# RWKV-6 attention with a hard-swish feed-forward on one core: the u sums of two chunks made wide, weights stored by partition, and a new instruction order

## The chip, the cores and the metric

One core of one Trainium2 chip runs the program. The metric is device time in microseconds; the runs of the kernel before are 543.66, 543.9 and 544.48 us, median 543.9 us.

## What is computed

The reference is a recurrence per batch entry and head, followed by a two-layer feed-forward over 3072 tokens:

```
batch, n_heads, seq, head_dim = (4, 8, 768, 48)
...
    for t in range(S):
        cur = np.einsum('bhd,bhe->bhde', u[None] * kt, vt)
        y[:, :, t] = np.einsum('bhd,bhde->bhe', rt, state + cur)
        state = wt[:, :, :, None] * state + np.einsum('bhd,bhe->bhde', kt, vt)
...
    h = x @ w_in
    g = h * np.clip(h + 3.0, 0.0, 6.0) / 6.0
    return (g @ w_out).astype(np.float32)
```

r, k, v, w and u are float32; w_in and w_out come as float64 and are sent to the core as 64-bit words.

## The kernel before

The sequence is cut into 24 chunks of 128 tokens (`L`), each of two halves of 64 (`HL`). Four chunks make a block of 512 tokens, so there are six blocks. Within a chunk the recurrence becomes matrix products:

- VectorE makes two running products of the decays (`back_scan`, L429, and `fore_scan`, L438) and with them scaled keys K (`make_k`, L449) and scaled reads R (`make_r`, L453).
- TensorE multiplies K by R for each half and head (`score`, L499). The part above the diagonal goes into the matrix A by a masked copy on VectorE (`above`, L506).
- The diagonal of A is the sum over d of r*k*u, which is what the reference's u term needs. For chunks 0 to 8, VectorE multiplies r by k (`own`, L462), TensorE multiplies by u (`own_dot`, L474: eight matmuls of 2 columns into a 128x8 tile), ScalarE copies the eight sums (`own_sum`, L480), and ScalarE scales the identity `eyes` by each of them (`diagonal`, L490, eight instructions of 128x64, in two steps of four).
- TensorE turns K (`turn_k`, L515; copied by `turned_k`, L520), adds keys times values to the state (`write`, L599; copied by `written`, L610, or L608 for chunk 1), and reads the old state (`read_state`, L577) and the values (`read_values`, L586) into y.
- For chunks 0 and 1 the last 16 rows of each head pair go round through x: `clear_y` (L650), `read_both` (the step "first"), `leave_last` on ScalarE (the step "third", L644 and L642), and `place_last` (L658, the step "read"). `leave_rest` copies y to x. For later chunks `leave` (L682) does it.

The feed-forward of block 0 is made directly (`up` L715, `ramp` L705, `gate` L726, `down` L734). For blocks 1 to 5 it goes by sums of parts and fewer products: sums of weights (`sum_w` and `sum_out`, L777 to L806) and of x (`sum_x`, the steps tx), products (L830), their reads on VectorE (L847) or ScalarE, `clip` (L851), a gate (L855), and the second layer (L885).

Weights arrive as 64-bit words in tiles `bits`, 768 KB at a time (`fetch`, L392, sixteen of them; w_in in three pieces of 2 KB for each partition, w_out in two of 3 KB). ScalarE makes two steps of each (`low_whole` L401, `high_sign` L406), VectorE two (`high_shift` L412, `high_low` L416, the step "full"). All loads of features, tokens and weights are issued by SyncE in one queue.

All of this is one order, written down as a table. `plan.add` names every step with its engine, a cost, what it must follow and which buffers it holds; `Plan.order` (L183) sorts the steps by the table `ORDER`, two characters for each step. Costs don't choose the order any more: they only give planned starts, and those decide how many filler matmuls `Plan.emit` (L231) puts before a TensorE step of the first 60 us (`spin`, L1257, 128 columns of the identity into a bank that nobody reads; four more stand ahead of everything). An engine runs its steps strictly in this order.

Of the kernel before, what the change touches and what calls it, by code (L numbers as in the profile page):

```python
# [31 lines left out]
ALONE = 4  # L32
LEAD = 5.403
# [49 lines left out]
    "AAADAIAQAKAOALANAPARASAYAVAjATAXAZAdAmAqAfAoAzA3A/ACAFAWAiAcAnAbAaAeAgAhAlAtAyAkApAxA1A5A9A8A+BNBUBcAJAMBIBfBSBaBRBF"  # L83
    "BJBTBVBXCGCLBpBvCBCRBdCYCdCnCyC7AUAvBjB4BuCABzBeBgBlBmBqCSCaCJCOCWCrCNCuC1E0DCDMDVDgBOBQCpC2DcDkCvCUCbCiDDDXDuDyC+DH"
    "DjFFDKFMFQFUFfFnFwCXDLC9DGEOEZDBDADRDWDsEKFzDZDqFPFWE5FZFeFkF3GVGXGlGfCcC4D9EJFmFpEEDYDwD+F2F5GYFlFvFoGNGPGSGiG0G5Do"
    "FxETFyF+GDEXEDFXFcGhGjG6F7GdF8GrGzG2HPHYHkH0HsEdGaF4GZGxG1F9FdGWGgHAHCHcGnHHGoHMHOHRH/IEIIFrG8FuGkG7HXHhGqGcGpHbHeIJ"
    "HVHiHWHyH2H9IrJWJlJtJ0GHHdGIG/HmItIyHGGtHNIPIVJcIDINIHIYIcKMLfLkG3IKG9HzILI/JCH3HZHjJeJjLnIvJbIwJgJiLxMAMLMWMQHnJdHo"
    "JvJ4K/LDJ1IBIdLqLuMIKTLtLwL1MRMfMmI4LlI6KHLmL6MBKOJUJnMFMPMpL4MJMbMiMwOvO9PEPLLHMGLKLrMHMZMeLyLZL0MtMxO5MYMrL9MvMzM6"
    "PJP+QKLSMnLVMNMoNANHMUL2MTO2PIQCM4O8M3PoPpPsQWQdQiQyQqNYO4NaOSO3PXPbOYN5OFQBQGQjPPQJPQQNQQQXQ5RIRQOCQEOEPhQDQcQgPlOg"
    "PRQrQwRUQbQvQeQxQ0Q1R3SoS1S6TCOHQkOKQIQlRERLQSPUQMRZRcSwQ+RWRARgRjRnTlUdUlRNRRRVRqRwSISNRvR/SOSuS9UiR7SzR8ULUNUPUvU9"  # L90
    "VOVUVYSCSvSETATWT+UCTISeSpUqUtVDTsUhTqUnUpUuVWVhVqSUUkSXTgUjU8VATkSyTGVCVKVsU1VHU6VLVPVVWAYTYVYjYZShVESnUrVFVbVfUxTL"
# [1510 lines left out]
```

## Time and profile before

| | |
|---|---|
| runs, us | 543.66, 543.9, 544.48 (median 543.9) |
| profiled execution, us | 544.22 |
| its span, first to last instruction | 542.5 us |
| TensorE busy | 533.3 us (98%) |
| VectorE, ScalarE, GpSimd busy | 425.6, 267.6, 113.1 us |
| granted TensorE clock | 0.999 of full |

The span is what the trace covers; the execution's own time is 1.7 us longer. Busy time of TensorE counts fillers, and the ends of its matmuls are modelled, so a wait that is shorter than the pipeline does not show as idle. Where a row reads "idle before, releaser", the engine had nothing until the named instruction ended.

### The profile page before, as it was taken

Reading aid. Unit: us, or ns where it says so; the run is one execution under the profiler, and the core shown is the slowest. Engines: PE = TensorE matmul, PEld = TensorE weight load, DVE = VectorE, ACT = ScalarE, POOL = GpSimd, SP = SyncE. Lnnn points to the kernel's source line nnn. Section 1 sums busy time; section 2 is a strip of 40 time slices with the busy share of each in tenths; the row PEclk is TensorE's granted clock in tenths of the full one; section 3 lists DMA queues with packets and bytes.
Section 4 is the critical chain, followed back from the end, with each engine's and each line's share of the span. In section 5 each row is a group of like instructions: output and inputs, shape, how many; then the busy total and the mean of one; then the engine's idle time right before and its main releaser. Section 6 shows DMA issues by size and latency. Waiting matters only on the chain.

```text
span 542.5 us, 13407 instructions
## 1 busy us (share of the span) xinstructions
PE 533.3 (98%) x5558; PEld 467.9 (86%) x5558; DVE 425.6 (78%) x726; ACT 267.6 (49%) x657; POOL 113.1 (21%) x111
## 2 busy tenths in 40 slices
PE   8999999999999999999999999999999999999995
PEld 8888876666878999888999888999888999888995
DVE  7889999768999977999977999968889624478531
ACT  4999894333664333556424657425454324264200
POOL 2000002456230135212513154115310000000000
PEclk9999999999999999999999999999999999999999
DMA  8959753333342343745145853032510001000001
GB/s 297 359 165 346 245 176 105 125 119 125 99 151 68 105 159 110 232 177 184 26 137 160 302 217 127 0 118 87 171 59 1 2 16 31 30 0 2 1 29 36
DMA packets 23670, 66.45 MB, mean 122 GB/s; under 512 B 3216, under 2 KB 10544, under 8 KB 23600
## 3 DMA queue, kind: packets, MB, share of 16 engines
q1 hardware_dynamic: 23472, 65.50, 35.4%
q8 instruction: 46, 0.75, 0.6%
q14 instruction: 24, 0.20, 0.1%
q10 hardware_dynamic: 128, 0.00, 0.0%
HBM read 59.69 MB, written 4.72 MB: 119 GB/s over the span
## 4 chain that ended last, share of the span: by engine, by line
PE 92%; DVE 6%; issue 1%; POOL 0%; ACT 0%; DVEq 0%; POOLq 0%
PE bank L885 29%; PE bank L830 24%; PE bank L715 8%; PE bank L734 8%; PE bankS L885 5%; PE bankS L830 4%; PE y_ps L577 2%; PE bankS L1261 2%; PE ps L515 2%; PE y_ps L599 2%; PE bank L499 2%; PE y_ps L586 2%; DVE g L847 2%; DVE g L855 1%; PE ps L474 1%
## 5 line engine op out<-in xcount | busy, mean ns | idle before, releaser
L851 ACT ACTIVATE clip<-g,three 128x512 f32<-128x512 f32 x80 | 57.1, 722 | 55.0 <-DVE g L847 45.3
L847 DVE TENSOR_TENSOR g<-bank,g 128x512 f32<-128x512 f32 x80 | 53.6, 684 | 10.0 <-PE bank L830 8.5
L855 DVE SCALAR_TENSOR_TENSOR g<-clip,g 128x512 f32<-128x512 f32 x80 | 56.5, 720 | 5.8 <-ACT clip L851 5.8
L885 PE MATMUL bank<-w_out,g 128*128 128x192 f32 x320 | 57.4, 328 | 0.0
L490 ACT ACTIVATE A<-eyes,dg 128x64 f32<-128x64 f32 x192 | 49.5, 338 | 10.9 <-PE y_ps L586 10.6
L885 PEld LDWEIGHTS bank<-w_out,g 128*128 128x128 f32 x320 | 52.8, 190 | 1.2 <-DVE g L855 0.3
L449 POOL TENSOR_TENSOR K<-feat_in,E 112x512 f32<-112x512 f32 x17 | 22.6, 1329 | 134.2 <-PE bank L499 128.4
L682 ACT COPY xT<-y_ps 48x256 f32<-48x256 f32 x88 | 32.1, 365 | 27.7 <-PE y_ps L586 26.9
L715 PE MATMUL bank<-xT,w_in 128*128 128x256 f32 (+1 forms) x216 | 45.5, 362 | 0.0
L734 PE MATMUL bank<-w_out,g 128*128 128x384 f32 x128 | 43.8, 491 | 0.0
L830 PE MATMUL bank<-xT,w_in 128*128 128x256 f32 x160 | 40.4, 381 | 0.1
L715 PEld LDWEIGHTS bank<-xT,w_in 128*128 128x128 f32 x216 | 36.6, 191 | 4.4
L845 ACT COPY g<-bank 128x512 f32<-128x512 f32 x50 | 28.8, 581 | 20.7 <-PE bank L830 17.2
L734 PEld LDWEIGHTS bank<-w_out,g 128*128 128x128 f32 x128 | 23.6, 190 | 14.1
L901 ACT ACTIVATE o<-bank 128x192 f32<-128x192 f32 x30 | 9.9, 329 | 49.8 <-PE bank L885 49.6
L830 PEld LDWEIGHTS bank<-xT,w_in 128*128 128x128 f32 x160 | 30.1, 190 | 4.4 <-ACT g L845 0.7
L429 DVE TENSOR_TENSOR_SCAN E<-feat_in,back 112x520 f32<-112x520 f32 x24 | 31.4, 1309 | 2.7 <-DMA feat_in<-in_feat_dram 1.7
L506 DVE COPY_PREDICATED A<-mask,bank 128x256 f32<-128x256 uint8 x48 | 18.6, 440 | 17.4 <-PE bank L499 17.3
L453 POOL TENSOR_TENSOR W<-feat_in,W 112x512 f32<-112x512 f32 x17 | 22.8, 1343 | 44.3 <-DVE W L438 44.3
L438 DVE TENSOR_TENSOR_SCAN W<-feat_in,start 112x520 f32<-112x520 f32 x24 | 31.4, 1309 | 0.6 <-PE y_ps L577 0.4
L830 PE MATMUL bank<-xT,bits 128*128 128x256 f32 x120 | 30.9, 382 | 0.2 <-DVE A L506 0.2
L885 PE MATMUL bank<-more,g 128*128 128x192 f32 x160 | 28.7, 329 | 0.0
(290 smaller groups left out, 1137.1 us busy)
## 6 DMA issues: line engine op xcount, KB each, us to landing
feat_in<-in_feat_dram SPq DMA_DIRECT2D x23, 772.5 KB, 4.4
bits<-in_moe_w_in_dram SPq DMA_DIRECT2D x8, 768.0 KB, 6.2
bits<-in_moe_w_out_dram SPq DMA_DIRECT2D x8, 768.0 KB, 4.9
feat_in<-in_moe_w_in_dram SPq DMA_DIRECT2D x8, 768.0 KB, 4.8
feat_in<-in_moe_w_out_dram SPq DMA_DIRECT2D x8, 768.0 KB, 4.7
rk_in<-in_tok_dram SPq DMA_DIRECT2D x15, 384.0 KB, 5.2
v_in<-in_tok_dram SPq DMA_DIRECT2D x24, 192.0 KB, 4.6
out_dram<-o SPq DMA_DIRECT2D x24, 192.0 KB, 2.1
```

The lines of the kernel that those rows point to most:

```text
L429: nc.vector.tensor_tensor_scan(out=E_[:, ::-1], data0=d["w"][:, :0:-1], data1=back.rearrange("q p t -> q (p t)")[:, ::-1], initial=0.0, op ...
L438: nc.vector.tensor_tensor_scan(out=W_, data0=d["w"][:, :-1], data1=starts[i % 2].rearrange("q p t -> q (p t)"), initial=0.0, op0=ALU.mult, ...
L490: nc.scalar.activation(out=d["A"][:, h, :], in_=eyes, func=ACT.Copy, scale=d["dg"][:, h])
L682: nc.scalar.copy(out=blocks[bk]["xT"][g * GP:g * GP + D, :, at:at + HL], in_=st[i]["y_ps"][a][(g ^ a) * GP:(g ^ a) * GP + D, :, :])
L715: nc.tensor.matmul(h_ps[:, :(c1 - c0) * L], lhsT=w_in[:, f // 2, j, f % 2, :], rhs=b["xT"][:, j, c0 * L:c1 * L], start=(j == 0), stop=(j = ...
L734: nc.tensor.matmul(b["o", c][:, :DM], lhsT=g_of(0, f, c), rhs=w_out[:, f, :], start=(f == 0), stop=(f == NFC - 1))
L830: nc.tensor.matmul(b["p", d, c][:, z * HB:(z + 1) * HB], lhsT=weight(W_PLACE[r], d)[:, z, :], rhs=x_at(bk, X_PLACE[r]), start=fresh and z ...
L845: nc.scalar.copy(out=out_, in_=src)
L847: nc.vector.tensor_tensor(out=out_, in0=src, in1=out_of(bk, d, other), op=ALU.add if sign > 0 else ALU.subtract)
L851: nc.scalar.activation(out=c, in_=out_of(bk, d, u), func=ACT.Relu, bias=three, scale=twice)
L855: nc.vector.scalar_tensor_tensor(out=g, in0=blocks[bk]["r", d, u], scalar=6.0, in1=g, op0=ALU.min, op1=ALU.mult)
L885: nc.tensor.matmul(b["d", p, to][:, :h], lhsT=a, rhs=w(), start=(f == 0 and k in (1, 5)), stop=(f == HF - 1 and k in (2, 3, 4)), skip_grou ...
```

## The change

Three things change in the program, and one in the order.

1. For chunks 0 and 1 (`BROAD`) the multiplication by u is made 128 columns wide: u is repeated 64 times, so that each sum stands in all 64 columns of its head. One VectorE multiplication by `eyes`, read out of PSUM, then makes the whole diagonal. ScalarE's copy and its eight scalings of these two chunks are gone.
2. The host stores w_in and w_out so that the 6 KB of a partition of one `fetch` lie together. Sizes are the same.
3. The rule for fillers: before a wait that is planned to be 1 us or more, fillers reach 0.3 us past the planned start, where they ended 0.12 us ahead of it before. The planner's costs are set to other numbers, and its transfer rate to 400 from 270.
4. `ORDER` is another table. `clear1` no longer waits for `kvs1`.

```
+BROAD = (0, 1)
 ORDER = (
-    "AAADAIAQAKAOALANAPARASAYAVAjATAXAZAdAmAqAfAoAzA3A/...
+    "AAACAHANAPARAMALAOAQAUAbASAWAYAaAjAqAdAoAvAzA+ADAE...
...
-    RATE = 270.0
+    RATE = 400.0
-    SPIN = ((6.3, 0.43), (1e9, 0.224))
-    FROM, UPTO = 3.0, 60.0
+    SPIN = ((7.2, 0.43), (1e9, 0.224))
+    FROM, UPTO, LONG = 3.0, 60.0, 1.0
...
-                while now < self.start[n] - 0.12:
+                room = -0.12 if self.start[n] < now + self.LONG else 0.3
+                while now < self.start[n] + room:
                     self.spin()
...
-                src = moe_w_in[:, f * 128:(f + 2) * 128].rearrange("(c p) (x j) -> p c x j", p=128, x=2)
+                src = moe_w_in[f // 2]
...
-                src = moe_w_out[f * 128:(f + 2) * 128, :].rearrange("(x p) (c j) -> p x c j", p=128, j=128)
+                src = moe_w_out[f // 2].rearrange("p x (c j) -> p x c j", j=128)
...
+        def broad_dot(i):
+            d = st[i]
+            d["dg_ps"] = pp.tile([L, P, 2, HL], F32, name="ps")
+            for p in range(P):
+                for a in range(2):
+                    half = slice(a * HL, (a + 1) * HL)
+                    nc.tensor.matmul(d["dg_ps"][half, p], lhsT=d["rk"][:, p, half],
+                                     rhs=u_col[:, p, :].rearrange("q (g o) -> q g o", o=1).to_broadcast([PR, 2, HL]),
+                                     start=True, stop=True)
+
+        def broad_diagonal(i):
+            d = st[i]
+            d["A"] = wk.tile([L, H, HL], F32, name="A")
+            nc.vector.tensor_mul(d["A"], d["dg_ps"].rearrange("s p g t -> s (p g) t"),
+                                 eyes.rearrange("s (o t) -> s o t", o=1).to_broadcast([L, H, HL]))
...
+            if i in BROAD:
+                plan.add(f"dot{i}", "PE", 0.95, do(broad_dot, i), [f"own{i}"], k + OWN, [("ps", [f"diag1{i}"])])
+            elif i < BY_PE:
...
+            if i in BROAD:
+                plan.add(f"diag1{i}", "DVE", 0.68, do(broad_diagonal, i), [f"dot{i}"] + [f"diag1{i - 1}"] * (i > 0), k + 0.6, [("A", [read_by(i)])])
...
-                plan.add(f"clear{i}", "PE", 0.5, do(clear_y, i), [f"kvs{i}", f"score{i}"], t, y)
+                plan.add(f"clear{i}", "PE", 0.95, do(clear_y, i), [f"kvs{i}"] * (i != APART) + [f"score{i}"], t, y)
...
-                plan.add(f"low{j}", "ACT", 0.83, do(low_whole, j), [f"fetch{j}"], t, [("more", [f"full{j}"])])
+                plan.add(f"low{j}", "ACT", 0.93, do(low_whole, j), [f"fetch{j}"], t, [("more", [f"full{j}"])])
...
-                plan.add(f"own{i}", "POOL", 2.2, do(own, i), [f"rkt{i}", "u"] + [f"own{i - 1}"] * (i > 0), k + 0.4,
+                plan.add(f"own{i}", "POOL", 2.4, do(own, i), [f"rkt{i}", "u"] + [f"own{i - 1}"] * (i > 0), k + 0.4,
...
-                plan.add(f"tx{bk}.{x}", "DVE", 0.335 * (X_PARTS[x + 1] - X_PARTS[x]), do(sum_x, bk, x),
+                plan.add(f"tx{bk}.{x}", "DVE", 0.44 * (X_PARTS[x + 1] - X_PARTS[x]), do(sum_x, bk, x),
...
-    laid["moe_w_in"] = _np.asarray(inputs["moe_w_in"])[rows]
+    w_in = _np.asarray(inputs["moe_w_in"])[rows]
+    laid["moe_w_in"] = w_in.reshape(nj, 128, -1, 2, 128).transpose(2, 1, 0, 3, 4)
+    laid["moe_w_out"] = _np.asarray(inputs["moe_w_out"]).reshape(-1, 2, 128, H * D).transpose(0, 2, 1, 3)
```

Line numbers of the changed kernel are some 2 to 24 higher: its narrow sums are L475, its wide sums L484, its VectorE diagonal L491, its fillers L1285.

SyncE's queue began with feat0 (the decays, then the rest), feat1, tok0, fetch0, tok1, fetch1, fetch2, feat2, and begins now with feat0, tok0, feat1, tok1, fetch2, fetch1, fetch0, feat2.

The first place is TensorE from the program's start. `ident` fillers are L1261 and L1285; `ps<-u_col,rk` is the u sum, `ps<-ident,K` the turning of K, `bank<-W,K` the scores. Before:

```order
L1261 MATMUL bankS<-ident 128x128 x17
L474 MATMUL ps<-u_col,rk 64x2 x8
L1261 MATMUL bankS<-ident 128x128 x3
L515 MATMUL ps<-ident,K 128x112 x4
L499 MATMUL bank<-W,K 64x64 x16
```

and now:

```order
L1285 MATMUL bankS<-ident 128x128 x12
L484 MATMUL ps<-u_col,rk 64x128 x8
L1285 MATMUL bankS<-ident 128x128 x4
L533 MATMUL ps<-ident,K 128x112 x4
L1285 MATMUL bankS<-ident 128x128
L517 MATMUL bank<-W,K 64x64 x16
```

Five fillers fewer stand before the first u sum, which is 128 columns wide instead of 2, and two more stand behind it. Over the whole program there were 17, 3, 2, 1, 3, 2, 3, 6 and 1 fillers in groups, 38 in all; there are now 12, 4, 1, 8, 2, 3, 1, 1 and 2, 34 in all. Up to the step read1 that is 37 before and 27 now.

The second place is VectorE after its constants, from the first scan on (`E<-feat_in,back` is the backward scan, `W<-feat_in,start` the forward scan, `rk` the product r*k, `top` and `w_in<-top,more` the steps shift and full). Before:

```order
L429 SCALAR_TENSOR_TENSOR E<-feat_in,back 112x520
L433 RECIPROCAL start_80<-E 112x8
L462 TENSOR_TENSOR rk<-feat_in 112x512
L438 SCALAR_TENSOR_TENSOR W<-feat_in,start_80 112x520
L449 TENSOR_TENSOR K<-feat_in,E 112x512
L506 COPY_PREDICATED A<-mask,bank 128x4x64 x2
L528 TENSOR_TENSOR S<-kvs,w_min 112x192
L453 TENSOR_TENSOR W<-feat_in,W 112x8x64
L544 TENSOR_TENSOR state_81<-S,kvs 112x192
L412 TENSOR_SCALAR top<-bits 128x768 x2
```

and now, from the product r*k of chunk 1 on:

```order
L463 TENSOR_TENSOR rk<-feat_in 112x512
L430 SCALAR_TENSOR_TENSOR E<-feat_in,back 112x520
L434 RECIPROCAL start_80<-E 112x8
L524 COPY_PREDICATED A<-mask,bank 128x4x64 x2
L413 TENSOR_SCALAR top<-bits 128x768
L450 TENSOR_TENSOR K<-feat_in,E 112x512
L491 TENSOR_TENSOR A<-ps,eyes 128x512
L546 TENSOR_TENSOR S<-kvs,w_min 112x192
L417 ISA w_in<-top,more 128x1536
L562 TENSOR_TENSOR state_81<-S,kvs 112x192
L439 SCALAR_TENSOR_TENSOR W<-feat_in,start_80 112x520
L413 TENSOR_SCALAR top<-bits 128x768
```

Both pieces are chunk 1. Its forward scan, and with it its R, stood right behind its backward scan and stand now behind the first finished piece of weights.

The third place is ScalarE from the copy of chunk 0's state part on (`more<-bits` are the steps low and sign, `kn<-ps` is turned, `xT<-y_ps` is third0). Before:

```order
L610 COPY kvs<-y_ps 112x384
L480 COPY dg<-ps 128x8
L490 ACTIVATE A<-eyes,dg 128x64 x8
L520 COPY kn<-ps 128x448
L401 ACTIVATE more<-bits 128x768
L406 ACTIVATE more<-bits 128x768
L644 COPY xT<-y_ps 48x128 x2
```

and now:

```order
L628 COPY kvs<-y_ps 112x384
L457 COPY w_min<-E 112x8
L402 ACTIVATE more<-bits 128x768
L407 ACTIVATE more<-bits 128x768
L402 ACTIVATE more<-bits 128x768
L538 COPY kn<-ps 128x448
L407 ACTIVATE more<-bits 128x768
L662 COPY xT<-y_ps 48x128 x2
```

Two pieces of weights, not one, now stand ahead of third0, and the scalings of the identity are gone.

## Rows read from the trace of the kernel before

**Rows 1.** The page's part 1: each engine's busy us, share of the span, instructions

```profile
PE 533.3 (98%) x5558; PEld 467.9 (86%) x5558; DVE 425.6 (78%) x726; ACT 267.6 (49%) x657; POOL 113.1 (21%) x111
```

**Rows 2.** Busy time by stretch: length, then each engine's busy us; clock, DMA share, GB/s

```profile
25.24:150.00 124.76, 124.52 (x1549) 94.28 (x1548) 109.08 (x212) 81.64 (x209) 30.39 (x27) 1.00 0.50 171
150.00:250.00 100.00, 99.25 (x939) 88.73 (x938) 90.35 (x136) 49.84 (x119) 26.61 (x24) 1.00 0.44 152
250.00:400.00 150.00, 149.37 (x1733) 136.31 (x1732) 128.65 (x204) 71.52 (x189) 51.67 (x46) 1.00 0.40 131
```

**Rows 3.** TensorE in order of time: start, length, line, tiles, records merged

```profile
7.49 0.63 PE L474 MATMUL ps<-u_col,rk 112*64 112x2 f32 x16
8.05 0.94 PE L1261 MATMUL bankS<-ident 128*128 128x128 f32 x6
8.82 0.55 PE L515 MATMUL ps<-ident,K 112*128 112x112 f32 x4
9.30 0.69 PE L499 MATMUL bank<-W,K 48*64 48x64 f32 x32
...
18.06 1.45 PE L658 MATMUL y_ps<-xT,S__115 112*128 112x64 f32 x12
...
23.80 1.60 PE L1261 MATMUL bankS<-ident 128*128 128x128 f32 x12
25.24 1.45 PE L658 MATMUL bank<-xT,S__115 112*128 112x64 f32 x12
```

**Rows 4.** The first fillers in two windows, 1.4 to 5.6 and 5.9 to 7.4

```profile
1.43 4.42 PE L1261 MATMUL bankS<-ident 128*128 128x128 f32 x19 [1.43 <-POOL ident masks.py:199]
...
5.65 1.91 PE L1261 MATMUL bankS<-ident 128*128 128x128 f32 x15
```

**Rows 5.** VectorE in order of time: chunk 0's product r*k, chunk 1's backward scan

```profile
6.38 0.67 DVE L462 TENSOR_TENSOR rk<-feat_in 112x512 f32<-112x512 f32 x1
...
8.99 1.24 DVE L429 TENSOR_TENSOR_SCAN E<-feat_in,back 112x520 f32<-112x520 f32 x1 [0.74 <-DMA feat_in<-in_feat_dram]
```

**Rows 6.** ScalarE in order of time, from chunk 1's scalings to third0

```profile
12.47 2.02 ACT L490 ACTIVATE A<-eyes,dg 128x64 f32<-128x64 f32 x8
14.39 0.52 ACT L520 COPY kn<-ps 128x448 f32<-128x448 f32 x1
14.80 1.09 ACT L401 ACTIVATE more<-bits 128x768 uint16<-128x768 uint32 x1
15.76 1.05 ACT L406 ACTIVATE more<-bits 128x768 bf16<-128x768 int32 x1
16.67 0.52 ACT L644 COPY xT<-y_ps 48x128 f32<-48x128 f32 x2
```

**Rows 7.** DMA issues at 2.2 us (tok0) and 3.2 us (tok1); last, us to landing

```profile
v_in<-in_tok_dram SPq DMA_DIRECT2D x1, 192.0 KB, 7.2
...
v_in<-in_tok_dram SPq DMA_DIRECT2D x1, 192.0 KB, 8.7
```

**Rows 8.** TensorE in order of time around 155 us, a wait and what follows

```profile
155.46 1.13 PE L830 MATMUL bank<-xT,apart 128*128 128x256 f32 x4 [0.46 <-DVE g L847]
156.42 1.03 PE L830 MATMUL bank<-xT,bits 128*128 128x256 f32 x4
```

**Rows 9.** Groups of VectorE, costliest first: busy us, mean ns, idle before

```profile
L847 DVE TENSOR_TENSOR g<-bank,g 128x512 f32<-128x512 f32 x80 | 53.6, 684 | 10.0 <-PE bank L830 8.5 <-ACT g L845 0.9
...
L429 DVE TENSOR_TENSOR_SCAN E<-feat_in,back 112x520 f32<-112x520 f32 x24 | 31.4, 1309 | 2.7 <-DMA feat_in<-in_feat_dram 1.7 <-POOL K L449 1.0
...
L726 DVE SCALAR_TENSOR_TENSOR g<-clip,bank 128x256 f32<-128x256 f32 (+1 forms) x36 | 13.4, 384 | 1.2 <-ACT clip L705 1.0
...
L482 DVE TENSOR_REDUCE dg<-rk 128x8 f32<-128x384 f32 x15 | 8.1, 542 | 1.3 <-ACT A L490 0.7 <-POOL rk L466 0.6
```

**Rows 10.** GpSimd's groups of the step own: busy us, mean ns

```profile
L466 POOL TENSOR_TENSOR rk<-rk,u_bc 128x384 f32<-128x384 f32 x15 | 20.2, 1346 | 1.2
L465 POOL TENSOR_TENSOR rk<-rk_in 128x384 f32<-128x384 f32 x15 | 18.8, 1250 | 38.3 <-DMA rk_in<-in_tok_dram 25.7 <-DVE dg L482 8.7 <-issue 3.9
```

More of the change, by code (lines that the diff above doesn't have):

```diff
@@ L87 @@
[L87 to L91, printed above, removed]
@@ L923, in refetch @@
                 t = io.tile([128, m], I64, name="feat_in")
-                src = (moe_w_in, moe_w_out)[which].rearrange("(p a) b -> p (a b)", p=128)
-                nc.sync.dma_start(out=t, in_=src[:, j * m:(j + 1) * m])
+                src = (moe_w_in[j].rearrange("p c x e -> p (c x e)"), moe_w_out[j].rearrange("p x e -> p (x e)"))[which]
+                nc.sync.dma_start(out=t, in_=src)
             seen[which, j] = t
@@ L1000, in fast_path @@
             behind = [f"fetch{BEHIND[i]}"] if i < len(BEHIND) and BEHIND[i] >= 0 else []
[L1001 removed]
+            plan.add(f"feat{i}", "SP", 0.45 if i else 1.15, do(load_feat, i), behind + [f"feat{i - 1}"] * (i > 0) + ["later"] * (i == 1), k - 20, kb=(1300 if i == 1 else 790) if i else 267,
                      hold=[("feat", [f"K{i}", f"R{i}"] + [f"own{i}"] * (i < BY_PE))])
[L1003 removed]
+            plan.add(f"tok{i}", "SP", 0.45, do(load_tok, i), behind + [f"feat{i}"] * (i > 1) + ["later"] * (i < 2), k - 19.9, kb=205,
                      hold=[("tok", [read_by(i)])])
             if i >= BY_PE:
[L1006 removed]
+                plan.add(f"rkt{i}", "SP", 0.45, do(load_rk, i), behind + [f"feat{i}"] * (i > 0), k - 19.8, kb=400,
                          hold=[("rk_in", [f"own{i}"])])
@@ L1089, in fast_path @@
                              [f"leave{i - 1}", f"leave{i}"], when(i) - 50, kb=1, dmas=3)
-        plan.add("u", "SP", 0.45, load_u, ["fetch3"], -60.0, kb=320)
-        plan.add("later", "SP", 0.45, load_rest, ["feat0"], key=-999.0, kb=630)
+        plan.add("u", "SP", 0.45, load_u, ["fetch3"], -60.0, kb=211)
+        plan.add("later", "SP", 0.45, load_rest, ["feat0"], key=-999.0, kb=524)
         for j in range(len(pairs)):
             t = CONV[0] + j * CONV[1]
-            plan.add(f"fetch{j}", "SP", 0.45, do(fetch, j), ["later"] * (j == 0), key=t - 20, kb=546 if f64 else 384,
+            plan.add(f"fetch{j}", "SP", 0.45, do(fetch, j), ["later"] * (j == 0), key=t - 20, kb=810 if f64 else 384,
                      hold=[("bits", [f"sign{j}", f"shift{j}"])] if f64 else ())
             if f64:
-                plan.add(f"low{j}", "ACT", 0.83, do(low_whole, j), [f"fetch{j}"], t, [("more", [f"full{j}"])])
-                plan.add(f"sign{j}", "ACT", 0.83, do(high_sign, j), [f"low{j}"], t)
+                plan.add(f"low{j}", "ACT", 0.93, do(low_whole, j), [f"fetch{j}"], t, [("more", [f"full{j}"])])
+                plan.add(f"sign{j}", "ACT", 0.91, do(high_sign, j), [f"low{j}"], t)
                 plan.add(f"shift{j}", "DVE", 0.48, do(high_shift, j), [f"fetch{j}"], t, [("top", [f"full{j}"])], port=True)
@@ L1245, in fast_path @@
             names = [f"vet{k}.{x}" for x in range(1 if which == "w" else 2)]
-            plan.add(f"refetch{k}", "SP", 0.45, do(refetch, which, j), [f"read{i}"], when(i), kb=820, hold=[("feat", names)])
+            plan.add(f"refetch{k}", "SP", 0.45, do(refetch, which, j), [f"read{i}"], when(i), kb=800, hold=[("feat", names)])
             for x, name in enumerate(names):
```

78 lines of the change are left out of this document (40 added, 38 removed).

## The prediction

> **What bounds the kernel now.** I read the page's totals first: TensorE is busy 533.3 us, 98% of the span [rows 1], so the end is TensorE's program, fillers included, plus what it waits. The windows then say where it waits: 0.24 us idle from 25 to 150 us, but 0.75 and 0.63 us in the two windows from 150 to 400 us, 1.4 us together [rows 2]. Nearly all the rest is 1.43 us before the first matmul [rows 4] and the tail, which this change leaves alone. Third, TensorE in order of time shows the start [rows 3]: the first real matmul, the u sum of chunk 0, begins at 7.49 us, and seven more groups of fillers follow up to read1 at 25.24 us, the shown ones of three (8.05) and six (23.80). Fillers are a fixed count: where data come sooner than planned, they cost time, and no idle time shows it. What the change can gain is therefore fillers and waits; TensorE's other work is the same but for the wide sums. The profiled execution took 544.22 us, 0.32 above the median of 543.9; I add the differences to the median.
>
> **The first fillers.** Nineteen of their records take 4.22 us (1.43 to 5.65), the other fifteen 1.84 us (5.65 to 7.49) [rows 3, 4]: 0.22 and 0.12 us each, TensorE at 1.2 and then at 2.4 GHz, though the granted clock reads 1.00 in the windows [rows 2]. Twelve fillers are 24 records: 5.65 + 5 x 0.12 = 6.25, and with 0.2 us to the next kind of work the first u sum starts at 6.45 instead of 7.49: **-1.0 us**. Its data are there: r*k stood behind the forward scan and began at 6.38 [rows 5]; it now follows the backward scan, one 1.2 us scan earlier, at about 5.2. If something else holds the u sum, the gain is lost: bound 0. Were all five fillers of the slower kind, which they are not, it would be 2.2.
>
> **The other fillers.** 21 before, 22 now, in eight groups each. One is 2 x 0.12 = 0.24 us; the group of six took 1.44 us [rows 3]. **+0.2 us.**
>
> **The wide u sums.** The narrow one took 0.56 us (7.49 to 8.05 [rows 3]) for 16 records. Wide, each record moves 128 columns, as a filler's does, 0.12 us. Lower bound: no dearer, 0.56. Upper bound: 16 x 0.12 = 1.9 us, one after the other. Which it is depends on whether the two halves of 64 output columns run side by side. The nearest row is the scores, also 64 output columns wide: 32 records of 64 columns in 0.62 us (9.30, and the next start at 9.92), where one after the other, at half a filler's 0.12, they would need 1.9. So I let the halves overlap: 8 x 0.12 = 0.95 us. Two chunks: **+0.8 us**, between 0 and +2.7. The Trainium skill (TensorEngine Tiling (Array Packing), Instruction Overhead) says that a matmul has about 60 cycles of overhead, so that one column costs as much as 60; by that rule, an estimate, 0.56 us becomes 0.56 x 128/60 = 1.2 us and the predicted time 0.5 us more, 543.4. The trace agrees in kind: 16 records of 2 columns took 0.56 us, 32 of 64 columns 0.62.
>
> **The diagonals.** ScalarE loses eight scalings, 2.02 us [rows 6], twice. VectorE gains two multiplications of 128x512 out of PSUM; the same form takes 684 ns elsewhere [rows 9], 1.4 us in all, partly where VectorE waited 0.74 us for feat1 [rows 5]. None of it is TensorE's; what it delays is in the waits below.
>
> **The queue and the weights.** tok0 now goes ahead of feat1, so feat1 lands where tok0 did, at 2.2 + 7.2 = 9.4 us, and the first weights land where tok1 did, at 3.2 + 8.7 = 11.9 us [rows 7], since the same bytes lie ahead. The new layout may take something off each transfer, and no step of TensorE waits for one, so I cost it at nothing. The cover was ScalarE: its first weight step began at 14.80 [rows 6], well behind the landing. That cover is gone, since ScalarE is free at 12.
>
> **The wait that takes its place.** third0 now stands behind two pieces of weights: 11.95, low 0.96, sign 0.91 (distances of the starts in [rows 6]); the second piece, which I let land 2.0 us after the first (one piece and tok1, 960 KB, landed in the 2.5 us from 9.4 to 11.9 [rows 7]); 14.0, low 0.96, turned 0.41, sign 0.91, third0 0.52: 16.8 us. TensorE reaches read0 at about 16.3: u sum 6.45 + 0.95, four fillers, turn 0.48 and one filler, scores at 9.1, state part at 9.7, second u sum at 10.3, clear at 11.3, eight fillers from 12.25, turn at 14.05, first0 at 14.5, chunk 1's state part at 15.7. So it waits 0.5 us for third0. Then up0.3.0 waits about 0.15 us for a bank that the scores of chunk 1 hold. **+0.65 us**, between 0 (the steps ahead are slower and cover it) and 1.5 (the weights land a microsecond later). Even so read0 comes at 16.8, where it was at 18.06, and read1 at about 24.7, with one more u sum done, where it was at 25.24 [rows 3]. Behind read1 there are seven fillers now and were one, which takes the lead back.
>
> **The waits behind 150 us.** Idle there is 1.4 us [rows 2]. Each wait also costs a refill: the four records behind the wait of 155 us took 1.13 us, the next four 1.03 [rows 8]; for the seven waits I count, 0.7 us. Together 2.1 us, the most that can be had. Waits come where a step takes longer than its planned cost: own on GpSimd is planned 2.2 us and takes 1.25 + 1.35 = 2.6 [rows 10], low 0.83 against 0.96 [rows 6]. The new table comes with costs nearer to these rows (2.4 and 0.93), so I take three quarters of the 2.1: **-1.6 us**, between -2.1 and, since every step has moved, +1.
>
> **Sum.** -1.0 + 0.2 + 0.8 + 0.65 - 1.6 = -0.95: **542.9 us**. The start alone is +0.65, and the chain above gives nearly the same: 0.5 us ahead at read1, one u sum (0.57) more done, six fillers (1.44) more to do. A difference of 0.2%, 1.1 us, is about what a measurement of this kernel tells from none, so the forecast lies just inside it.
>
> **Rivals.**
> (a) *The order is no better behind 150 us.* The old waits go and as many new ones come. For it: every step moved, and VectorE works 90 of 100 us there [rows 2]. Against: the costs are nearer to the rows. Time: 543.9 + 0.65 = 544.5, from 543.4 to 545.5.
> (b) *Slower: the second layer of block 0 waits for VectorE.* The new order leaves six pieces of the first layer (up0.1.2, 6.2, 14.2, 8.2, 4.2 and 2.2) to the reads of chunks 5 to 7, and down0.2.1, at some 120 us, needs the gate of up0.2.2, with only read7 between them. Ahead of that gate VectorE has a backward scan (1.31 us), a sum of GpSimd's product (0.54) and two other gates (0.38 each) [rows 9], 2.6 us. It decides as soon as VectorE ends that gate later than TensorE ends read7; then TensorE waits for what is left, up to 2.6 us: 542.9 + 2.6 = 545.5. Against: VectorE is busy only 109 of 125 us up to 150 [rows 2].
> (c) *The start is covered and every late wait goes.* No 0.65, and -2.1 for -1.6: 541.7.
> That the layout does nothing to the transfers is possible and changes no number, as long as they stay hidden.
>
> **How the numbers follow.** Forecast 0.52, (a) 0.25, (b) 0.11, (c) 0.12. The forecast's own range is 541.8 to 544.1, and half of it lies below 542.8; with (c) and a little of (a) faster gets 0.40. Slower is most of (b), a fifth of (a) and a remainder: 0.16. Same: 0.44. The range goes from 541.0, just past (c), to 545.3, which leaves out most of (b) and the end of (a), and takes in half of the wide sums' upper bound.
>
> **What would show it.** First u sum at 6.3 to 6.6 us, 0.9 to 1.0 us long; 1.9 us means that the halves don't overlap. read0 at 16.6 to 17.0 with third0 as its releaser, read1 at 24.4 to 25.0. Idle time of 0.3 to 0.7 us from 150 to 400 us; 1.4 or more is (a). A gap before a second-layer product at 115 to 125 us is (b). The prediction is wrong if the time lies outside its range, and its reasons are if the start is not some 0.65 us worse and the later part some 1.6 us better.

## The result and the profile after

The changed kernel takes 547.25 us (median of six runs, 546.44 to 548.67) where the kernel before, on the same chip, took 544.59. The ratio is 1.0049, 95% interval 1.0034 to 1.0065: 2.7 us slower (1.9 to 3.5). The forecast was 542.9 us, 1.0 us faster than the median of before, with a range up to 545.3. The profiled execution took 547.24 us with a span of 545.5, 3.0 us more than the span of before.

The page's totals of the changed kernel, to set beside [rows 1]:

```profile
PE 534.1 (98%) x5550; PEld 465.5 (85%) x5550; DVE 427.4 (78%) x728; ACT 265.1 (49%) x639; POOL 109.1 (20%) x111
```

TensorE's own program hardly changed. Added up over the trace from each start to the next, all fillers take 10.56 us, of which 0.70 are waits behind them, instead of 11.65 without any, and all u sums 6.02 instead of 5.07: 0.85 us less together, waits left out. So the loss is waiting. Busy time by stretch, as in [rows 2] (length, then TensorE, its weight loads, VectorE, ScalarE, GpSimd; then granted clock, DMA share, GB/s):

```profile
25.24:150.00 124.76, 123.91 (x1535) 93.33 (x1535) 108.37 (x215) 80.26 (x199) 27.66 (x26) 1.00 0.47 166
150.00:250.00 100.00, 99.54 (x942) 88.73 (x941) 90.89 (x133) 49.10 (x117) 28.82 (x26) 1.00 0.46 157
250.00:400.00 150.00, 148.44 (x1725) 134.32 (x1724) 127.57 (x211) 72.59 (x189) 46.73 (x43) 1.00 0.38 128
```

The granted clock is 1.00 throughout. TensorE is idle 0.85 us from 25 to 150 us (0.24 before), 0.46 from 150 to 250 (0.75 before) and 1.56 from 250 to 400 (0.63 before), where the forecast had 0.3 to 0.7 us for the last two stretches together. Before 25.24 us it is idle 1.3 us, not counting the fixed 1.43 at its head; before it was 0.3.

The start, TensorE in order of time (to compare with [rows 3, 4]):

```profile
1.43 4.46 PE L1285 MATMUL bankS<-ident 128*128 128x128 f32 x24 [1.43 <-POOL ident masks.py:199]
6.46 1.11 PE L484 MATMUL ps<-u_col,rk 112*64 112x128 f32 x16 [0.56 <-DVE rk L463]
...
17.11 1.52 PE L676 MATMUL y_ps<-xT,S__115 112*128 112x64 f32 x12 [0.35 <-ACT xT L662]
...
24.82 1.45 PE L676 MATMUL bank<-xT,S__115 112*128 112x64 f32 x12
```

Twelve fillers, the first u sum at 6.46 us, read0 at 17.11 behind ScalarE's third0 (xT), read1 at 24.82: the forecast had 6.45, 16.8 and 24.7. The wide u sum takes 1.03 us (to the next start, 7.49). What was not forecast is the wait of 0.56 us for r*k, whose data landed 0.6 us later than before. It is in this execution alone: five of the kernels below (after_start, moves_first, checks_late, checks_all, checks_moves) have the same start and no such wait, and their first u sum begins at 5.80 to 6.39 us, their read1 at 24.34 to 24.46. From 25 to 150 us they are idle 0.28 to 0.54 us, not 0.85. The first u sum of checks_moves:

```profile
5.80 1.11 PE L484 MATMUL ps<-u_col,rk 112*64 112x128 f32 x16
```

The fillers themselves differ from one execution to the next. At a granted clock of 1.00 their first records take 0.21 us each and the later ones 0.11, and in the fourteen traces between 12 and 27 of them are slow. In the seven traces with the old start the first u sum begins at 7.13 to 8.21 us (7.49 in the kernel before), so a single pair of executions tells the gain of the start only to about a microsecond.

Why third0 is late shows in ScalarE's order of time:

```profile
15.06 0.53 ACT L538 COPY kn<-ps 128x448 f32<-128x448 f32 x1 [0.89 <-PE ps L533]
...
16.45 0.52 ACT L662 COPY xT<-y_ps 48x128 f32<-48x128 f32 x2
```

ScalarE had both pieces of weights in time (10.85 and 12.74 us) and waited 0.89 us for TensorE's second turn of K, whose copy stands ahead of third0.

Behind 150 us the waits that the kernel before had at 155, 161 to 163, 301, 329 and 375 us are gone. In their place, by the excess of one start over the usual step, stand 0.63 us at 232, 0.34 at 305, 0.46 at 312, 0.26 at 318 and 1.14 at 386. All five end on VectorE. So the next view is VectorE's: its groups from 150 to 400 us, where the last number is idle time just before the group and what ended it. `word_min`, `word_max` and `w_max` are the range checks (`vet`): each of 22 pieces of weights, 768 KB, is fetched again (`refetch`) into a buffer of the chunks' and reduced; only the flag at the program's end needs their results. Before:

```profile
L934 DVE TENSOR_REDUCE word_max<-feat_in 128x1 f32<-128x768 f32 x16 | 15.1, 943 | 0.0
L934 DVE TENSOR_REDUCE word_min<-feat_in 128x1 f32<-128x768 f32 x15 | 14.1, 941 | 0.0
L931 DVE TENSOR_REDUCE w_max<-feat_in 128x1 f32<-128x1536 f32 x6 | 10.4, 1741 | 0.0
```

After:

```profile
L952 DVE TENSOR_REDUCE word_min<-feat_in 128x1 f32<-128x768 f32 x16 | 15.2, 947 | 4.8 <-DMA feat_in<-in_moe_w_in_dram 3.1 <-DMA feat_in<-in_moe_w_out_dram 1.7
L952 DVE TENSOR_REDUCE word_max<-feat_in 128x1 f32<-128x768 f32 x16 | 15.1, 944 | 2.7 <-DMA feat_in<-in_moe_w_out_dram 2.7
...
L949 DVE TENSOR_REDUCE w_max<-feat_in 128x1 f32<-128x1536 f32 x6 | 10.5, 1745 | 0.8 <-DMA feat_in<-in_wflat_dram 0.8
...
L795 DVE SCALAR_TENSOR_TENSOR T__4401<-xT 128x256 f32<-128x256 f32 x2 | 1.3, 630 | 0.8 <-DMA xT<-xT 0.8
```

In the old order VectorE never stands before a check; in the new one it stands there 8.3 us, and 0.8 us more before the partial sums of x (L795). With each group's share, VectorE's idle time that a transfer ended is 0.2 us before and 9.15 us after. Did the transfers slow down? DMA issues of these pieces from 150 to 400 us (KB each, median us from issue to landing), before:

```profile
feat_in<-in_moe_w_in_dram SPq DMA_DIRECT2D x8, 768.0 KB, 4.8
feat_in<-in_moe_w_out_dram SPq DMA_DIRECT2D x8, 768.0 KB, 4.7
feat_in<-in_wflat_dram SPq DMA_DIRECT2D x6, 768.0 KB, 4.3
```

and after:

```profile
feat_in<-in_moe_w_in_dram SPq DMA_DIRECT2D x8, 768.0 KB, 5.0
feat_in<-in_moe_w_out_dram SPq DMA_DIRECT2D x8, 768.0 KB, 4.7
feat_in<-in_wflat_dram SPq DMA_DIRECT2D x6, 768.0 KB, 4.2
```

They did not. (The chunks' own loads of 772.5 KB did, from 4.2 to 5.7 us in the median, but no idle time of VectorE ends on them there.) What changed is what the planner allows the pieces: 0.45 us for the issue, the bytes at its rate, and 1.9 us to land. That was 0.45 + 820/270 + 1.9 = 5.4 us for a piece with nothing ahead of it, above the medians (and up to 8.8 us with others ahead), and is 0.45 + 800/400 + 1.9 = 4.35 us for 18 of the 22 pieces, below the medians of w_in and w_out; twelve of the 22 took longer than that. By the plans in the two kernels, 12 of the 22 first checks stood within 1.1 us of the planned landing before and 15 do now (within 0.5 us 5 and 9), so for most checks this allowance is nearly all the slack that they have. And the median is not the end of it: a piece whose issue has others ahead of it takes longer.

```profile
feat_in<-in_moe_w_in_dram SPq DMA_DIRECT2D x1, 768.0 KB, 7.8
```

This one, issued at 299.05 us behind two transfers for chunk 19 and ahead of the next chunk's, needed 7.8 us; 4.0 us is the shortest of the 22. The Trainium skill (SBUF — State Buffer, The DMA setup-cost knee) gives a transfer about 2 us fixed and the bytes at 436 GB/s, for 768 KB an estimate of 3.8 us; the trace agrees within 0.2 us for the shortest, not for one in a queue.

VectorE works in order, so an unlanded check holds the gates behind it. The last of the five waits is of the same kind, with a transfer that is not a check's. For chunks 18 and 19, SyncE issues two steps `move` of three 16 KB transfers each, which bring parts of xT together (the small pairs of the texts below); the second stands behind two large transfers of chunk 23. VectorE, TensorE and that DMA issue:

```profile
383.37 0.88 DVE L795 SCALAR_TENSOR_TENSOR T__4401<-xT 128x256 f32<-128x256 f32 x1 [0.84 <-DMA xT<-xT]
384.29 1.11 DVE L795 SCALAR_TENSOR_TENSOR T__4401<-xT,T__4401 128x256 f32<-128x256 f32 x1
385.43 1.11 DVE L797 TENSOR_TENSOR T__4401<-T__4401,xT 128x256 f32<-128x256 f32 x1
```

```profile
387.05 1.13 PE L848 MATMUL bank<-T__4401,bits 128*128 128x256 f32 x4 [0.98 <-DVE T__4401 L795]
```

```profile
xT<-xT SPq DMA_DIRECT2D x3, 16.0 KB, 4.5
```

Three transfers of 16 KB take 4.5 us to land, VectorE waits 0.84 us for them, its sums take 0.9 to 1.1 us each, and TensorE waits 0.98 us for the partial sum.

### The profile page after: what moved, and what is told of

It reads as the page before. It is cut to its first block, busy times and chain, and to the rows that moved or that the text cites. A ratio compares the mean times of both kernels' runs of the same rounds, so it can differ in the third digit from the quotient of the medians.

```text
span 545.5 us, 13347 instructions
## 1 busy us (share of the span) xinstructions
PE 534.1 (98%) x5550; PEld 465.5 (85%) x5550; DVE 427.4 (78%) x728; ACT 265.1 (49%) x639; POOL 109.1 (20%) x111
## 4 chain that ended last, share of the span: by engine, by line
PE 83%; DMA 8%; DVE 5%; issue 1%; ACT 1%; SPq 0%; POOL 0%; DVEq 0%
PE bank L903 26%; PE bank L848 24%; PE bank L752 8%; PE bank L733 6%; PE bankS L903 5%; PE bankS L848 4%; DMA feat_in<-in_moe_w_in_dram 3%; PE bank L517 2%; PE y_ps L617 2%; PE y_ps L595 2%; PE y_ps L604 2%; PE ps L533 2%; DMA bits<-in_moe_w_out_dram 1%; DMA feat_in<-in_moe_w_out_dram 1%; DMA feat_in<-in_feat_dram 1%
## 5 line engine op out<-in xcount | busy, mean ns | idle before, releaser
L873 DVE SCALAR_TENSOR_TENSOR g<-clip,g 128x512 f32<-128x512 f32 x80 | 54.1, 694 | 6.4 <-ACT clip L869 6.3
L508 ACT ACTIVATE A<-eyes,dg 128x64 f32<-128x64 f32 x176 | 45.0, 336 | 6.7 <-PE y_ps L604 6.4
L903 PE MATMUL bankS<-w_out,g 128*128 128x192 f32 x160 | 28.6, 327 | 0.0
## 6 DMA issues: line engine op xcount, KB each, us to landing
feat_in<-in_feat_dram SPq DMA_DIRECT2D x23, 772.5 KB, 6.0
```

The costliest lines, as they stand in the source:

```text
L508: nc.scalar.activation(out=d["A"][:, h, :], in_=eyes, func=ACT.Copy, scale=d["dg"][:, h])
L873: nc.vector.scalar_tensor_tensor(out=g, in0=blocks[bk]["r", d, u], scalar=6.0, in1=g, op0=ALU.min, op1=ALU.mult)
L903: nc.tensor.matmul(b["d", p, to][:, :h], lhsT=a, rhs=w(), start=(f == 0 and k in (1, 5)), stop=(f == HF - 1 and k in (2, 3, 4)), skip_grou ...
```

## The experiments

**Theory A**: the loss is in waits that the new order makes, most of them where VectorE stands before a transfer. **Rival B**: it is made in the start, and the late waits follow from it. **Rival C**: the new layout slows the transfers. Times are medians of 6 to 12 runs; "above before" is from the ratio to before on the same chip, with its 95% interval.

**layout_only.** The kernel before with the weights stored by partition:

```
-                src = moe_w_in[:, f * 128:(f + 2) * 128].rearrange("(c p) (x j) -> p c x j", p=128, x=2)
+                src = moe_w_in[f // 2]
...
-                src = moe_w_out[f * 128:(f + 2) * 128, :].rearrange("(x p) (c j) -> p x c j", p=128, j=128)
+                src = moe_w_out[f // 2].rearrange("p x (c j) -> p x c j", j=128)
```

> The kernel before with the weights laid out by partition and nothing else; order, fillers and sums as before. Theory A (the loss comes from waits that the new order makes): no difference, within 0.5 us of before. Rival C (the new layout moves the weights in a way that slows or crowds the other transfers): 1 to 2.7 us slower, with the first weights landing at another time than 11.4 us and new waits for transfers behind 150 us.

544.7 us, ratio 0.9995 (0.9986 to 1.0005): no difference. C falls.

**after_start and after_late.** Two orders spliced from the two tables, as lists of steps:

```
after_start: the changed kernel; its steps up to the first TensorE step planned at 118 us, then the rest in the order of before
after_late:  the kernel before;  its steps up to the first TensorE step planned at 266 us, then the rest in the changed order
```

> The changed kernel with its own order up to about 120 us and the order of before behind that (wide sums, diagonals on VectorE, layout and fillers stay changed). Theory A (about two thirds of the loss are waits that the new order makes behind 150 us): 0.6 to 1.2 us slower than before, with no wait of over 0.5 us behind 300 us that the kernel before hadn't. Rival B (the loss is made in the start, and the late waits only follow from it): 2.2 to 3 us slower, as the changed kernel.

> The kernel before, narrow sums and all, with its own order up to about 265 us and the changed kernel's order behind that. Theory A: 1.4 to 2.2 us slower than before, with the wait for the partial sum of the fifth block at about 383 us back. Rival B: within 0.5 us of before.

after_start: 545.72 us, 1.0 us above before (0.4 to 1.7). after_late: 546.98, 1.5 above (1.0 to 2.1). Each as A has it, and together they give nearly the 2.7, though neither has the changed order from 118 to 266 us. The changed kernel has it, and is 1.6 us further above before than after_start. B falls: the late waits come with the late order, on the start of before too. They even show how a check's wait becomes TensorE's. The same place at 314 to 319 us, first in the changed kernel, VectorE and TensorE:

```profile
314.13 0.95 DVE L952 TENSOR_REDUCE word_max<-feat_in 128x1 f32<-128x768 f32 x1 [1.89 <-DMA feat_in<-in_moe_w_out_dram]
...
318.34 0.68 DVE L865 TENSOR_TENSOR g<-bank,g 128x512 f32<-128x512 f32 x1
```

```profile
317.95 1.03 PE L848 MATMUL bank<-xT,apart 128*128 128x256 f32 x4
319.07 1.13 PE L848 MATMUL bank<-T__3567,bits 128*128 128x256 f32 x4
```

and in after_late (its profiled execution, 548.19 us, is the longest of its twelve):

```profile
314.52 0.95 DVE L934 TENSOR_REDUCE word_max<-feat_in 128x1 f32<-128x768 f32 x1 [3.42 <-DMA feat_in<-in_moe_w_out_dram]
...
318.09 0.65 DVE L847 TENSOR_TENSOR g<-g 128x512 f32<-128x512 f32 x1
```

```profile
316.80 1.03 PE L830 MATMUL bank<-xT,apart 128*128 128x256 f32 x4
319.39 0.91 PE L830 MATMUL bank<-T__3589,bits 128*128 128x256 f32 x3 [1.57 <-DVE g L847]
```

VectorE waits 1.53 us longer for the piece (3.42 and 1.89), and from start to start TensorE takes 2.59 us (316.80 to 319.39) instead of 1.12 (317.95 to 319.07), 1.47 more. What such a place costs is therefore not fixed: it is what the transfer is late beyond the slack, and it changes when the steps ahead move. It changes without that too: at 232 us, with the same steps ahead, TensorE loses 0.63 us in the changed kernel, 1.37 in moves_first and 1.28 in checks_late. The wait for the partial sum is back as well, 1.41 us at 386.

**moves_first.** One step of SyncE:

```
-move4.1.1  feat23  rkt23  move4.1.0
+move4.1.1  move4.1.0  feat23  rkt23
```

> The changed kernel with one step of SyncE moved: the last pair of small transfers of the fourth block (16 KB each) goes ahead of two transfers of chunk 23 that stand before it. Theory A (the wait of 1.14 us at 385.75 us is the small transfer's landing behind the large ones): the small transfers land by 379.5 instead of 383.35 us, VectorE begins the partial sum 0.84 us sooner, when its scan of chunk 22 ends, and the wait shrinks to some 0.3 us; 1.9 us slower than before, where the changed kernel was 2.7 slower. Rival: another step of VectorE is late instead, and the time stays 2.7 us above before.

547.29 us, 3.1 above before (1.7 to 4.4; the eleven runs reach from 545.90 to 553.11). The interval takes in the 1.9 of A as well, so it is the trace that decides, and there the rival was right. The small transfers landed at 379.44 us and the wait at 386 was gone, but chunk 23's transfers and the checked piece behind them landed later, the check stood in front of an output step, and TensorE waited there. VectorE and TensorE:

```profile
386.19 0.95 DVE L952 TENSOR_REDUCE word_max<-feat_in 128x1 f32<-128x768 f32 x1 [0.78 <-DMA feat_in<-in_moe_w_out_dram]
387.06 0.35 DVE L921 SCALAR_TENSOR_TENSOR o<-bank,o 128x192 f32<-128x192 f32 x1
```

```profile
385.47 1.13 PE L848 MATMUL bank<-T__4401,bits 128*128 128x256 f32 x4
387.46 1.73 PE L903 MATMUL bank<-more,g 128*128 128x192 f32 x9 [0.86 <-DVE o L921]
```

0.78 us for the piece, 0.86 us of TensorE. While checks without slack stand in VectorE's queue, making one transfer early makes another late.

**checks_late.** Nine pieces and their checks leave the dense stretch:

```
-refetch13 to refetch21 issued from 292 us on, their 18 checks from 299 to 393 us among the gates, sums and scans
+refetch13 to refetch21 issued from 378 us on, their checks from 435 to 487 us, the flag's steps behind them; all others in place
```

> The changed kernel with nine of the 22 pieces of weights that are fetched again for the range checks, and the two checks of each on VectorE, moved from 290 to 400 us to behind 430 us; every other step keeps its place. Theory A (VectorE works in order, stands before checks whose transfers have not landed, 6.75 us behind 250 us, and the gates and partial sums behind them hold TensorE): the waits at 305, 312, 318 and 386 us go or stay under 0.3 us, and the time is 1.0 to 1.7 us above before instead of 2.7; the wait at 232 us stays. Rival (the partial sums are slow beside GpSimd's work, whatever the checks do): the waits of 305 and 386 us stay, 2.2 to 2.7 us above before.

545.95 us, 0.9 above before (0.4 to 1.4). The checks that are left from 250 to 400 us:

```profile
L952 DVE TENSOR_REDUCE word_max<-feat_in 128x1 f32<-128x768 f32 x3 | 2.8, 946 | 0.0
L952 DVE TENSOR_REDUCE word_min<-feat_in 128x1 f32<-128x768 f32 x3 | 2.8, 946 | 0.3 <-DMA feat_in<-in_moe_w_in_dram 0.3
```

```profile
250.00:400.00 150.00, 148.99 (x1731) 135.94 (x1730) 113.63 (x187) 72.80 (x189) 46.99 (x43) 1.00 0.27 91
```

TensorE is idle 1.01 us there instead of 1.56. The waits of 312 and 318 us are gone and that of 305 is down to 0.2, as A has it; that of 232 us stays, at 1.28. The one of 384 us stayed, 1.14 us, which A had wrong and the rival right, because the small transfers still stood behind the large ones (VectorE waits 0.8 us for xT). The shift also takes 14 us of VectorE's work out of that stretch (113.63 for 127.57), so this run alone does not part late transfers from a full VectorE.

**wide_only.** The kernel before with the wide u sums and their diagonals on VectorE in chunks 0 and 1:

```
+BROAD = (0, 1)
...
-sum0, diag00, diag10 (ScalarE), sum1, diag01, diag11 (ScalarE)
+diag10, diag11 (VectorE) where sum0 and sum1 stood
```

> The kernel before with the wide u sums and VectorE diagonals of chunks 0 and 1 and nothing else: old layout, order and rule for fillers (which now sets one filler more). Theory A (TensorE's program is the bound, so what it is given to do is paid): two sums 0.47 us longer and a filler, 1.2 us, and since the diagonal holds the one PSUM buffer in which the next turn is made, up to 0.5 us of wait there: 1.0 to 1.7 us slower than before. Rival (the start has fillers and waits enough to cover it): within 0.4 us of before.

545.93 us, 1.25 above before (0.8 to 1.7), as A has it. TensorE:

```profile
7.03 1.10 PE L484 MATMUL ps<-u_col,rk 112*64 112x128 f32 x16 [0.20 <-DVE rk L463]
...
9.29 0.55 PE L533 MATMUL ps<-ident,K 112*128 112x112 f32 x4
```

The sum takes 1.04 us (to 8.07), and the turn of K begins at 9.29 behind five fillers, where it began at 8.82 behind three [rows 3]: the buffer `ps` is a single one, the diagonal reads it, and the plan fills the wait. By itself the wide sum costs what TensorE is given to do; in the changed kernel the fillers, 1.8 us less with waits left out, pay for it.

**tuned_a and tuned_b.** The kernel before with orders found by moving single steps behind 60 us as long as the planned end fell, with 0.7 us more allowed for each late transfer, and the last ten pieces of checks behind 420 us.

```
-ORDER of before
+two other orders behind 60 us
```

> The kernel before, narrow sums and old layout, with the steps behind 60 us put in another order, in which the late transfers are allowed 0.7 us more than the old plan's rate gives a lone one, GpSimd's products 2.6 us, and the last ten range checks stand behind 420 us. Theory A: VectorE's waits for transfers are none and TensorE's idle time from 150 to 400 us falls from 1.4 us to under 0.6: 0.6 to 2 us faster than before. Rival (the waits come from durations that no plan has right): within 0.5 us of before.

> As tuned_a with another order found in the same way: the same expectations; the two together show how far such orders scatter when the plan calls them equal.

tuned_a: 550.35 us, 5.6 above before (4.7 to 6.5). tuned_b: 545.12, 0.3 above (-0.2 to 0.8). A had both faster, and neither is: tuned_a is clearly slower, tuned_b is the rival's case. The plan in the kernels puts their ends 0.2 us apart; they differ by 5 us. Moving everything opened waits that no transfer makes, such as this one of tuned_a, where TensorE stands for ScalarE's copy of the state part:

```profile
104.23 0.67 PE L577 MATMUL y_ps<-W,S 48*48 48x64 f32 x32 [1.43 <-ACT kvs L610]
```

**splice.** tuned_b without its first part:

```
-tuned_b from 60 us on
+the order of before up to 100 us, tuned_b from there
```

> The kernel before up to about 100 us in its own order, and the order of tuned_b behind that, so without the wait of 0.87 us at 81.6 us that tuned_b made. Theory A: idle time of TensorE from 250 to 400 us 0.2 us instead of 0.6, 0.3 to 1.3 us faster than before. Rival (the waits come back elsewhere): within 0.3 us of before.

544.72 us, ratio 0.9998 (0.9989 to 1.0007): no difference, the rival's case. TensorE's idle time from 250 to 400 us is the 0.17 us that was expected, but 1.14 us stand from 150 to 250, 0.91 of them in one wait for a gate at 155 us.

**checks_all.** From checks_late on, the pieces that VectorE stood before around 231 us move too, and the first small pair goes ahead of chunk 23:

```
-refetch7, refetch9, refetch5 planned from 220 to 225 us, their checks from 224 to 230
+planned now: refetch5 222, vet5 230; refetch7 301, vet7 305 and 311; refetch9 358, vet9 363 and 383 us; the other checks settle around them
-tok22  move4.1.1  feat23  rkt23  move4.1.0
+move4.1.0  tok22  feat23  rkt23  move4.1.1
```

> As checks_late, and besides the checks of the pieces that VectorE stood before at 231 us are moved to later places and the two last pairs of small transfers of the fourth block go ahead of chunk 23's large ones. Theory A (what is left of the late loss in checks_late are its two waits of 1.28 us at 231 and 1.14 us at 384): both go, VectorE waits under 1.5 us for transfers behind 150 us, and the time is 0.4 to 2.0 us below checks_late, from 1.1 us faster than before to 0.5 slower. Rival (each wait that goes only moves to the next late step): 0.5 to 1.5 us slower than before.

544.59 us, ratio 0.9999 (0.9989 to 1.0009): the 2.7 us are gone, with the wide sums, the layout, the fillers and the order of nearly all other steps as changed.

```profile
150.00:250.00 100.00, 100.00 (x943) 89.17 (x942) 87.33 (x130) 50.00 (x118) 27.23 (x25) 1.00 0.40 141
250.00:400.00 150.00, 148.91 (x1731) 136.10 (x1730) 117.98 (x190) 72.05 (x190) 48.25 (x44) 1.00 0.30 102
```

From 150 to 250 us TensorE never waits. The wait of 382 us stayed, because only one of the two small pairs was ahead; VectorE:

```profile
380.33 0.76 DVE L795 SCALAR_TENSOR_TENSOR T__4370<-xT 128x256 f32<-128x256 f32 x1 [1.03 <-DMA xT<-xT]
```

**checks_moves.** One step more:

```
-move4.1.0  tok22  feat23  rkt23  move4.1.1
+move4.1.0  move4.1.1  tok22  feat23  rkt23
```

> As checks_all, and the second pair of small transfers, which still stood behind chunk 23's three large ones and landed at 380.31 us, goes ahead of them. Theory A: both pairs land by 376.5 us, VectorE begins the partial sum at 379.3 us, when its scan of chunk 22 ends, not at 380.33, and TensorE's wait of 1.2 us at 382.5 falls to 0.2: 0.6 to 1.4 us faster than before. Rival (the slow partial sums, 0.8 to 1.1 us each beside GpSimd's work, or the next step are late instead): within 0.5 us of before.

543.38 us, ratio 0.9974 (0.9965 to 0.9983): 1.4 us faster than before (0.9 to 1.9) and some 4 us faster than the changed kernel, from moving the checks, the flag and two steps `move`, with what settled around them. The second pair lands in 1.8 us, where the pair behind the large transfers took 4.5:

```profile
xT<-xT SPq DMA_DIRECT2D x3, 16.0 KB, 1.8
```

VectorE begins its sums as soon as its scan ends, and TensorE, whose row shows no idle time, loses 0.2 us at the place instead of 1.2:

```profile
379.22 0.40 DVE L795 SCALAR_TENSOR_TENSOR T__4370<-xT 128x256 f32<-128x256 f32 x1
...
380.31 1.29 DVE L797 TENSOR_TENSOR T__4370<-T__4370,xT 128x256 f32<-128x256 f32 x1
381.63 1.23 DVE L795 SCALAR_TENSOR_TENSOR T__4370<-xT,T__4370 128x256 f32<-128x256 f32 x1
```

```profile
382.91 1.13 PE L848 MATMUL bank<-T__4370,bits 128*128 128x256 f32 x4
```

Its windows, TensorE idle 0.30, 0.00 and 0.09 us:

```profile
25.24:150.00 124.76, 124.46 (x1538) 94.13 (x1537) 108.61 (x216) 80.23 (x199) 28.52 (x27) 1.00 0.46 166
150.00:250.00 100.00, 100.00 (x943) 89.13 (x942) 87.73 (x131) 49.99 (x118) 27.65 (x25) 1.00 0.41 141
250.00:400.00 150.00, 149.91 (x1736) 136.98 (x1735) 118.36 (x191) 72.84 (x190) 49.00 (x44) 1.00 0.30 102
```

VectorE's idle time before transfers from 150 to 400 us is still 4.5 us here. It costs TensorE next to nothing (0.09 us idle): behind the two longest of these waits, 1.44 us at 223 and 1.73 at 367, VectorE comes to wait for TensorE again (0.46 us at 228, 2.06 at 371).

**narrow_start.** The kernel before up to about 142 us, the order of checks_moves behind it (some steps between 90 and 260 us, at the seam, and three checks behind moved again):

```
-the rest of before's order
+the rest of checks_moves' order
```

> The kernel before (narrow sums, old layout, its own order up to about 142 us) with the order of checks_moves behind that. Theory A (start and late part add up: the start of before is 1.0 us better, the late part of checks_moves 0.5 to 1.5 better than that of before): 0.5 to 2 us faster than before. Rival (the order behind a start must be the one it was searched with): 0 to 3 us slower, with waits between 140 and 260 us.

544.09 us, ratio 0.9984 (0.9974 to 0.9995): 0.9 us faster than before (0.3 to 1.4), inside A's wide range, but not faster than checks_moves, as it would be if start and late part added up. After_start's 1.0 us had said that the start of before is the better one; put in front of the good late part it shows no gain, though TensorE is idle 0.44 us from 150 to 250 here and not at all in checks_moves. How much of the 2.7 us belongs to the start is so known only to about a microsecond.

## Why the prediction was wrong

**The first and the other fillers** (-1.0 and +0.2): right in kind, and the number is luck. The first u sum began at 6.46 us for 6.45, but its fillers had ended at 5.89 and the wait for r*k made up the difference; without that wait the five other executions begin at 5.80 to 6.39. The 0.2 us to the next kind of work is not in the rows either: the 1.84 us of the fifteen records reach to the start of the u sum. All fillers took 1.8 us less, waits left out, for the 0.8 forecast; how much of it is the varying number of slow records stays open.

**The wide u sums** (+0.8): right in kind, 0.1 low. They took 1.03 us each, not 0.95, 0.94 us more in all; the halves of 64 columns do overlap (1.9 us without). The Trainium skill (TensorEngine Tiling (Array Packing), Instruction Overhead) gave an estimate of 1.2 us by its rule; the row lies between the two, nearer to the forecast.

**The start's waits** (+0.65): the wait came, at read0 and with third0 as its releaser (0.35 us idle for 0.5), but by another path. The forecast had third0 behind weights that land at 11.9 and 14.0 us; they landed at 10.85 and 12.74. What held ScalarE is its copy of the turned K, which waits for TensorE's own turn, so read0 follows that turn by 2.7 us in all six traces (14.41 and 17.11 here, 13.76 and 16.45 in checks_moves). That read0 was forecast to within 0.3 us and read1 to 0.1 is in part luck. The wait for r*k was not in it. For the start as a whole after_start has 1.0 us (0.4 to 1.7), for the forecast's 0.65.

**The layout** (nothing): right, by layout_only.

**The waits behind 150 us** (-1.6, bounds -2.1 and +1): this step failed. It took three quarters of 2.1 us because "the new table comes with costs nearer to these rows". For own and low that is so, and the old waits did go. But the same table has another cost in it, the transfers', which fell from 5.4 to 4.35 us for a piece that takes 4.2 to 5.0 in the median and up to 7.8; I read the new rate only for the start, where no step waits, and never asked which engine stands before a late transfer. What the runs show in its place is +1.5 us (after_late, 1.0 to 2.1; the changed kernel less after_start gives 1.6), beyond the upper bound of +1, which the interval just reaches. Against -1.6 that is 3.1 us, nearly all of the 3.7 between the forecast 1.0 us faster and the measured 2.7 slower.

**Rival (a)** had the form of it, old waits gone and new ones in their place, and too low a price. It gave as many new waits as old. There came fewer, five for the seven it counted, but longer ones: 2.8 us by the excess of starts, for 2.1. Its argument against, costs nearer to the rows, was the mistake itself. **Rival (b)** did not come: no gap at 115 to 125 us, and the longest idle time from 25 to 150 us is 0.4 us, at 44 us. **Rival (c)** is where checks_moves goes, with most of its late waits gone: 1.4 us faster than before, not 2.2, and with the start's cost still in it.

The cause is shown as far as this: with the checks and the small transfers of one block elsewhere, and nothing else undone, the loss is gone (checks_all) and turns into a gain (checks_moves); where the late order is put on the start of before, it comes back (after_late). That it is the late transfers, not VectorE's load, is shown for the small pair alone, whose move took nothing from VectorE (0.9999 to 0.9974); for the checks it is argued from the kernel before, which has the same checks in the same stretch, no wait before them and less TensorE idle time there. The plan in the kernels, worked through again, points the same way, though it is no run: at the rate of 400, with 2.4 us to land instead of 1.9 (some 4.9 us for a lone piece, where the medians are 4.2 to 5.0), TensorE's planned waits from 150 to 400 us grow from 0.45 to 3.0 us in the changed order, but only from 0.6 to 0.8 in that of before and from 0.45 to 0.7 in that of checks_moves. That the planner's rate made the search set the checks so close is argued from the two tables and their allowances; no search with the old rate was made.

## What to carry to other kernels

When a hand-written or searched order is made again with new costs, set each new cost beside the spread of the measured durations, not beside the fastest: a search uses up whatever slack a cost leaves, and a transfer that shares its queue has a long tail. Then look for engines that work in order and stand before a transfer, and at what stands behind them; work that nobody waits for, such as a check, belongs where its engine is idle, not ahead of work that holds the bottleneck. A wait that is moved by moving one transfer ahead of another is not gone until the other one has slack too. And before a wait is put down to a change, look for it in other executions of the same steps: the wait for r*k was in one trace of six.

## What the runs showed of the hardware

The time from issue to landing of a small transfer goes by what stands ahead of it: three of 16 KB took 1.8 us behind none and 4.5 us behind transfers of 384 and 772.5 KB. The Trainium skill (SBUF — State Buffer, Can I just issue two DMAs to hit both halves?) says that all of a kernel's transfers land on the same 16 DMA engines and that two at once serialize; the two rows agree.

VectorE's sums of two 128x256 operands take 0.42 us in most places. From 379 to 387 us three of four took 0.6 to 1.3 us each in the changed kernel and in checks_moves (the other 0.40 to 0.43), while GpSimd ran a scaling of the state and three products there. The planner's 0.44 us has nothing of that; in checks_moves the four sums together took 3.5 us and were early enough all the same.
